# Gated linear attention feeding a squared-ReLU feed-forward layer: ten weight subtractions on GpSimd, three crossing copies on ScalarE, and a new order for the first phase

## The chip, the cores and the metric

One Trainium2 chip, one of its cores. The metric is the device time of one execution in microseconds (us). A core has five engines that run their own queues: TensorE (PE in the rows; its weight loads are PEld), VectorE (DVE), ScalarE (ACT), GpSimd (POOL) and SyncE (SP), which only issues DMAs here. They wait for each other through semaphores.

## The reference

```python
# q, k, v, f_logit: (4 batches, 8 heads, 768 steps, 48), float32
f = 1.0 / (1.0 + np.exp(-f_logit))
for t in range(S):
    state = f[:, :, t, :, None] * state + np.einsum('bhd,bhe->bhde', k[:, :, t], v[:, :, t])
    y[:, :, t] = np.einsum('bhd,bhde->bhe', q[:, :, t], state)
x = y.transpose(0, 2, 1, 3).reshape(3072, 384)
h = x @ w_in                       # 384 -> 2048
r = np.maximum(h, 0.0)
out = (r * r) @ w_out              # 2048 -> 384
```

## The kernel before, in words

Time is cut into 6 blocks of 128 steps, so a block has 512 tokens over the 4 batches. The attention of a block is done in four units, one for each pair of heads; unit n belongs to block n // 4. A unit turns the recurrence into matrix products of 64 steps: VectorE makes running products of the gates with two scans, scales keys and queries by them, and TensorE makes scores, state updates and outputs with many small matmuls. The fourth unit of a block has no keys and queries of its own: heads have 48 rows where a unit has 2 x 64, so the last pair of heads is held in the spare rows of the other three. The output y of a unit is stored as two parts, a high one of the matmul's type (float32r) and the rest, and so are the weights.

The feed-forward layer has 16 slices f of 128 hidden features. For each slice and block, layer 1 is nine matmuls of 128x512 (three input tiles, three products of high and lower parts), then ScalarE does ReLU, square and a copy to the high part `gh`, VectorE subtracts it to get `gl`, and layer 2 is nine matmuls more. The weights come as 64-bit words that are decoded on the chip: two ScalarE passes, a shift-or and a sign-or on VectorE, a ScalarE copy to the high part and a subtraction `w[:, 1] = a - w[:, 0]` for the lower part (`halves`, line 172 copy, line 174 subtraction).

The order of the first phase is written out by hand, in the strings `FIRST` and `SECOND`. Each word is a step, a letter and a number, and `step()` issues it; all instructions of an engine then run in the order of the words. In the first phase the kernel does the attention of blocks 0 and 1 (units 0 to 7), decodes twelve early weights (slices 0 to 5, both layers) and does slices 0 to 5 for block 0. After it a regular flow of 16 slices a block runs. The letters that matter here:

- for a unit: `G` gates (ScalarE, line 446), `K` scan and scaled keys, `Q` the same for queries, `T` four TensorE transposes of the keys, `N` their copy out of PSUM (ScalarE), `S` scores, `D` state updates, `M` the causal mask (VectorE, line 596), `C` the states (VectorE, lines 611 and 618), `Y` the outputs (64 small matmuls, lines 631 and 640), `H` the high part of y (ScalarE, line 660), `z` its subtraction on TensorE (block 0), `X` the lower part (line 674 or 676), `r` and `s` the crossing copies
- the crossing copies: a product of one head may need queries (`rx`, step `r`) and states (`sx`, step `s`) on the other half of the partitions. `across()` (line 486) moves them, by a ScalarE copy or by a DMA of SP's queue. Before, all `r` of block 1 and `s5` to `s7` are DMAs
- `A I V c J` are the five decode steps of a layer-1 weight and `B O Z d P` those of a layer-2 weight. `J` and `P` are the subtractions. `e n t a w` decode the rows of the fourth unit
- `u` is layer 1 for a slice with the first three input tiles, `U` adds the fourth (slices 0 and 1 only) or is the whole (slices 2 to 5), `R` ReLU, square and high part, `E` the lower part (line 264), `W` layer 2 (line 274)
- `g` and `h` move the rows of the fourth unit into the other input tiles, on GpSimd's and SP's DMA queues (line 683); slices 2 and later need them
- `busyN` are N transposes whose result nobody reads (line 805): fill for TensorE

GpSimd does little in this phase: two small maximum steps inside each `K` (line 456), the DMA issues of `m` and `g`, and in the later flow block transposes (line 535). Its queue was not in the set of engines that keep the order by hand, but its order was settled by the tile scheduler.

Of the kernel before, what the change touches and what calls it, by code (L numbers as in the profile page):

```python
# [13 lines left out]
F32 = mybir.dt.float32  # L14
# [29 lines left out]
Q = 32  # L44
# [20 lines left out]
LAST_AT = ((-6, 0, "v"), (1, 1, "s"))  # L65


FIRST = """
j0 e0 n0 f0 busy11 busy3 G0 busy2 k0 t0 K0 T0 f1 k1 Q0 G1 v0 K1 S0 N0 D0 M0 i0 A0 I0 T1 L2 o2 L4 C0
Q1 r0 s0 G2 K2 v1 Y0 N1 H0 z0 X0 D1 S1 B2 i3 Q2 T2 busy3 m1 C1 a0 S2 A3 w0 v2 o1 N2 r1 D2 G4 I3 i1  # L70
M1 s1 K4 v3 A1 Y1 D3 H1 C2 s2 z1 X1 r2 m0 f5 m2 S3 r3 o0 B0 V0 M2 k5 L6 v5 busy3 Y2 H2 Q4 r4 v4 C3 s3
G5 I1 T4 z2 X2 M3 busy9 Y3 c0 N4 K5 G6 Q5 V1 H3 busy5 z3 X3 T5 S4 D4 o3 i5 o5 i2 B3 J0 m4 r5 B1 C4 c1 s4 u0
O0 U0 M4 Y4
"""
SECOND = """
J1 Z0 u1 V3 R0 K6 H4 X4 N5 D5 S5 E0 T6 d0 P0 A2 C5 c3 U1 O1 I2 W0 R1 N6 J3 M5 h3 Z1 d1 s5
Y5 Q6 H5 X5 V2 c2 E1 g3 U3 P1 A5 v6 o4 S6 D6 M6 i4 J2 r6 C6 m5 I5 R3 E3 A4 W1 V5 O3 I4 c5 J5 U2 R2
m6 O2 V4 Z2 s6 v7 r7 Y6 H6 c4 X6 E2 J4 U5 d2 D7 S7 P2 U4 M7 C7 Z3 B4 B5 R4 s7 W2 O4 O5 d3 Z4 Z5 d4
d5 P3 Y7 E4 H7 X7 g7 h7 P4 R5 E5 W3 W4 P5 W5
"""  # L80


class Moe:


    def __init__(self, ctx, tc, const, sums, out):
        self.tc, self.nc, self.sums, self.out = tc, tc.nc, sums, out

        self.const, self.raw, self.w, self.ps, self.turns = const, {}, {}, {}, 0
        self.xs, self.spares, self.w4, self.homes, self.held = [], 0, None, {}, None  # L90

        self.floor = const.tile([P, 1], F32, name="floor")
        tc.nc.vector.memset(self.floor, -31.0 / 64.0)

# [73 lines left out]
        yield from self.halves(self.w[f, i], a)  # L168

    def halves(self, w, a):  # L170
        nc = self.nc
        nc.scalar.copy(out=w[:, 0], in_=a)  # L172
        yield
        nc.vector.tensor_tensor(out=w[:, 1], in0=a, in1=w[:, 0].bitcast(F32), op=ALU.subtract)
        yield

    def decode_any(self, f, i, scr):
# [188 lines left out]
def fast_path(ctx, psum, tc, moe, ident, low, flag, fkqT, vN, w, w4, out):  # L366
    nc = tc.nc
    V, G = nc.vector, nc.gpsimd
# [32 lines left out]
    def weights_load(f, i, mark=False):  # L401
        raw = moe.words(f, i)
        if mark:

            V.memset(raw.bitcast(I32)[0:1, 0:1], 0)
        nc.sync.dma_start(raw, w[f, i])

    class Unit:
# [79 lines left out]
        def crossed(self):  # L488
            self.rx = self.wk([ROWS, B * C], "rx", 2)
            for c in range(self.blk == 0, NC):  # L490
                r = (1 - c) * C
                self.across(
                    self.rx[c * C : c * C + D].rearrange("p (b t) -> p b t", t=C),
                    self.ra[r : r + D].rearrange("p (b c t) -> p b c t", b=B, c=NC)[:, :, c],
                    self.blk == 1,
                )

        def crossed_states(self):
            for c in range(self.blk == 0, NC):
                r = (1 - c) * C  # L500
                self.across(self.sx[c * C : c * C + D], self.sp[r : r + D, c], self.blk == 1 and self.hp > 0)

        def turn(self):

# [26 lines left out]
        def turn_blocks(self):  # L531

            for a in range(0, P, Q):
                for r in range(0, P, Q):
                    ins = G.tensor_copy(  # L535
                        out=self.kn[a : a + Q, :, r : r + Q], in_=self.kb[r : r + Q, :, a : a + Q]
                    ).ins
                    for t in ticks[-1:]:
                        tc.add_manual_dep(ins, t.name, mybir.DependencyInfo(
                            mybir.DependencyClass.NoSync, mybir.DependencyReason.SCHED_ONLY  # L540
                        ), reason="behind the last slot")

        def turned(self):
            if self.n < TURNED:
# [177 lines left out]
    )  # L722
    half = list(range(LO)), list(range(LO, NF))
    xs = {blk: moe.new_x(blk, blk) for blk in range(2)}
    units, decoding, shared, ticks = {}, {}, [], []

    for t in xs[0]:
        G.memset(t[C + 32 :].bitcast(F32), 0.0)
# [10 lines left out]
    def slot(old, new):  # L739

        ab = ps_a.tile([P, 2, 512], F32, tag="ab", name=f"ab{(new or old).nm}_{new is None}")
        rows = [[], []]
        if old:
            old.py = ab[:, :, : B * C]
            for c in range(NC):
                for b in range(B):
                    for part in range(2):  # L750
                        for h in (c, 1 - c):
                            rows[c].append((C, lambda a=(part, b, c, h): old.output_one(*a)))
        if new:
            new.sd = ab[:, :, B * C :]
            new.dd = shared[0].rearrange("p (c e) n -> p c (e n)", c=NC)[:, :, : B * D]
            adds = [
                [] if new.last_of(c) else [
                    (D, lambda a=(b, c, h): update(*a)) for b in range(B) for h in (c, 1 - c)
                ] for c in range(NC)
            ]  # L760
            for h in range(2):
                for b in range(B):
                    for c in (h, 1 - h):
                        rows[h].append((C, lambda a=(b, c, h): new.score_one(*a)))
            rows = [adds[0] + rows[0], rows[1] + adds[1]]
        seen = []

        def behind(ins, first):
            tc.add_manual_dep(ins, first.name, mybir.DependencyInfo(
                mybir.DependencyClass.Sync, mybir.DependencyReason.DATA  # L770
            ), reason="one bank")

        def update(b, c, h):
            ins = new.add_one(new.dd, b, c, h).ins
            if c == 0 and b == B - 1 and h:

                seen.append(G.memset(tick, 0).ins)  # L777
                ticks.append(seen[0])
                behind(seen[0], ins)
            elif c and b == 0 and h:  # L780
                behind(ins, seen[0])

        at = [0, 0]
        while any(rows):
            r = min((r for r in range(2) if rows[r]), key=lambda r: at[r])
            cols, do = rows[r].pop(0)
            at[r] += cols
            do()

    def step(t):  # L790

        nm = t.rstrip("0123456789")
        n = int(t[len(nm) :])  # L800
        if nm == "busy":
            if 0 not in moe.cur.ph:
                moe.bank(0)
            for _ in range(n):
                nc.tensor.transpose(out=moe.cur.ph[0][:, 0:P], in_=ident, identity=ident)
        elif nm in ("i", "o"):
            weights_load(n, "io".index(nm))
        elif nm == "j":
            nc.sync.dma_start(moe.fourth_words(), w4)
        elif nm in "entaw":  # L810
            if nm == "e":
                decoding["fourth"] = moe.decode_fourth()
            next(decoding["fourth"])
        elif nm in "AIVcJBOZdP":
            i = "AIVcJBOZdP".index(nm) // 5
            if nm in "AB":
                decoding[n, i] = moe.decode(n, i, pro, True)
            next(decoding[n, i])
        elif nm == "u":
            moe.up(n, last=False)  # L820
        elif nm == "U" and n < SPLIT:
            moe.up_fourth(n)
        elif nm == "U":
            moe.up(n)
# [12 lines left out]
    pro = early.enter_context(tc.tile_pool(name="pro", bufs=1))  # L837
    minus = pro.tile([ROWS, ROWS], F32R, name="minus")
    nc.scalar.activation(minus, ident[:ROWS, :ROWS], AF.Copy, scale=-1.0)
    with tc.manual_schedule(engines={ET.PE, ET.SP, ET.DVE, ET.Activation}):  # L840
        with tc.tile_pool(name="ps_p", bufs=2, space=bass.MemoryType.PSUM) as ps_p:
            for t in FIRST.split():
                step(t)
# [3 lines left out]
        for t in SECOND.split():  # L847
            step(t)
# [307 lines left out]
```

## Time and profile before

| what | us |
|---|---|
| median of 3 runs (482.86 to 484.52) | 483.9 |
| the profiled execution's own time | 485.53 |
| its span, first to last instruction | 483.8 |
| TensorE busy, 4759 matmuls | 469.5 |
| VectorE busy, 483 instructions | 262.6 |
| ScalarE busy, 561 instructions | 277.4 |
| GpSimd busy, 226 instructions | 84.8 |

The granted clock of TensorE is 0.994 of the full 2.4 GHz over the span. A busy time is the union of an engine's instructions. TensorE's ends are modelled, so instructions overlap in its rows and a wait can lie inside a busy stretch: start-to-start times tell more.

### The profile page before, as it was taken

The page shows a single profiled execution, that of the slowest core. Times are in us where ns is not written, and L with a number is a line of the kernel's source. Part 1 is how long each engine was busy: PE and PEld are TensorE (multiplying, and loading weights), DVE is VectorE, ACT ScalarE, POOL GpSimd, SP SyncE. Part 2 cuts the span into 40 slices and gives each one's busy share as a digit, 9 for nine tenths or more (in the row PEclk, how much of TensorE's full clock was granted, in tenths as well). Part 3 has the DMA queues.
Part 4 walks back from the last instruction along what each step waited for, and adds up shares of the span by engine and source line. Part 5 has one row for each costly group of instructions (what it writes and reads, how often), then busy time and mean ns, then how long its engine had stood idle before and what let it go on. Part 6 is the DMA issues. An engine that isn't in the chain of part 4 may idle for free. (4 is left out here: it accounts for less than half of the span.)

```text
span 483.8 us, 11562 instructions
## 1 busy us (share of the span) xinstructions
PE 469.5 (97%) x4759; PEld 385.8 (80%) x4759; DVE 262.6 (54%) x483; ACT 277.4 (57%) x561; POOL 84.8 (18%) x226
## 2 busy tenths in 40 slices
PE   5888999999999999999999999999999999999996
PEld 5766778888888888888888888888888888888884
DVE  7997995898978447543457453356453312221111
ACT  4785676878758556545546645555654444544441
POOL 6222010001011404150053250052350000000000
PEclk9998999999999999999999999999999999999999
DMA  8983417467204205332005232004300002100002
GB/s 294 311 251 94 131 31 243 161 216 262 60 13 159 84 3 125 95 94 81 3 2 127 94 93 84 1 0 106 114 12 3 2 0 34 66 0 2 1 0 70
DMA packets 22636, 42.60 MB, mean 88 GB/s; under 512 B 4512, under 2 KB 8128, under 8 KB 22576
## 3 DMA queue, kind: packets, MB, share of 16 engines
q1 hardware_dynamic: 22128, 40.86, 27.7%
q0 software_dynamic: 448, 0.92, 0.7%
q8 instruction: 39, 0.64, 0.6%
q14 instruction: 21, 0.17, 0.1%
HBM read 31.69 MB, written 4.72 MB: 75 GB/s over the span
## 5 line engine op out<-in xcount | busy, mean ns | idle before, releaser
L247 PE MATMUL ph<-x,w 128*128 128x512 f32 x864 | 216.3, 395 | 0.0
L247 PEld LDWEIGHTS ph<-x,w 128*128 128x128 f32 x864 | 161.0, 189 | 34.5 <-DVE gl L264 0.3
L274 PE MATMUL po<-gh,w 128*128 128x512 f32 x570 | 175.5, 389 | 0.0
L264 DVE TENSOR_TENSOR gl<-ph,gh 128x512 fp32r<-128x512 f32 x95 | 65.4, 689 | 157.6 <-ACT gh L259 157.3
L257 ACT ACTIVATE ph<-ph 128x512 f32<-128x512 f32 x96 | 55.9, 583 | 127.0 <-PE ph L247 126.8
L274 PEld LDWEIGHTS po<-gh,w 128*128 128x128 f32 x570 | 107.0, 188 | 22.2
L274 PE MATMUL po<-gl,w 128*128 128x512 f32 x285 | 111.2, 390 | 0.0
L274 PEld LDWEIGHTS po<-gl,w 128*128 128x128 f32 x285 | 53.5, 188 | 11.2
L258 ACT ACTIVATE ph<-ph 128x512 f32<-128x512 f32 x96 | 55.9, 582 | 3.0
L259 ACT CAST gh<-ph 128x512 fp32r<-128x512 f32 x95 | 55.8, 587 | 3.0
L535 POOL COPY turn<-turn 32x128 f32<-32x128 f32 x112 | 42.1, 376 | 8.3 <-DVE turn L527 3.7
L456 POOL TENSOR_SCALAR fkq<-fkq 128x8 f32<-128x8 f32 x18 | 12.8, 714 | 141.9 <-DVE fkq L451 119.3
L451 DVE TENSOR_TENSOR_SCAN fkq<-fz,dr 128x520 f32<-128x520 f32 x18 | 22.3, 1238 | 6.7 <-ACT fz L446 6.6
L172 ACT CAST w<-wa 128x384 fp32r<-128x384 f32 (+1 forms) x33 | 16.6, 512 | 14.9 <-DVE wa L159 11.7
L465 DVE TENSOR_TENSOR_SCAN fkq<-fz,dz 128x520 f32<-128x520 f32 x18 | 22.4, 1247 | 0.6
L631 PE MATMUL ab_False<-sc,vn 64*48 64x64 f32 (+1 forms) x480 | 20.7, 220 | 0.0
L676 DVE TENSOR_TENSOR x<-ab_False,x 112x512 fp32r<-112x512 f32 x12 | 8.3, 692 | 21.6 <-ACT x L660 21.6
L660 ACT CAST x<-ab_False 112x512 fp32r<-112x512 f32 x12 | 7.0, 587 | 22.5 <-PE shared L566 17.6
L144 ACT ACTIVATE wa<-raw 128x384 f32<-128x384 f32 (+1 forms) x33 | 18.1, 549 | 2.4 <-DMA raw<-in_w_dram 2.4
L640 PE MATMUL ab_False<-rx,sx 48*48 48x64 f32 (+1 forms) x240 | 19.4, 216 | 0.0
L777 POOL MEMSET flag<- 1x1 int32 x16 | 1.4, 88 | 102.4 <-PE shared L566 100.4
L155 DVE SCALAR_TENSOR_TENSOR wa<-raw,wa 128x384 int32<-128x384 int32 (+1 forms) x33 | 18.0, 552 | 0.7
(148 smaller groups left out, 499.3 us busy)
## 6 DMA issues: line engine op xcount, KB each, us to landing
raw<-in_w_dram SPq DMA_DIRECT2D x32, 384.0 KB, 3.8
fkq<-in_fkqT_dram SPq DMA_DIRECT2D x15, 768.0 KB, 5.4
vn<-in_vN_dram SPq DMA_DIRECT2D x24, 192.0 KB, 4.7
out_dram<-ob SPq DMA_DIRECT2D x14, 256.0 KB, 2.2
fkq<-in_fkqT_dram SPq DMA_DIRECT2D x9, 256.0 KB, 4.5
x<-ys SPq DMA_DIRECT2D x30, 64.0 KB, 2.3
last_kq<-fkq SPq DMA_DIRECT2D x28, 64.5 KB, 2.3
out_dram<-part SPq DMA_DIRECT2D x3, 256.0 KB, 2.6
```

The costliest lines, as they stand in the source:

```text
L144: nc.scalar.activation(a, upper_f, AF.Abs, scale=2.0**-112, **kw)
L247: self.nc.tensor.matmul(self.cur.ph[f], lhsT=w[:, i], rhs=x[:, j], start=first and n == 0, stop=last and n == 2)
L257: nc.scalar.activation(ph, ph, AF.Relu)
L258: nc.scalar.activation(ph, ph, AF.Square)
L259: nc.scalar.copy(out=gh, in_=ph)
L264: self.nc.vector.tensor_tensor(out=gl, in0=self.cur.ph.pop(f), in1=gh.bitcast(F32), op=ALU.subtract)
L274: self.nc.tensor.matmul(c.po[e], lhsT=l, rhs=r, start=f == c.fs[0] and i == 0, stop=f in c.ends and i == 2, skip_group_check=len(c.ends) > 1,)
L451: V.tensor_tensor_scan(out=rr[:, ::-1], data0=self.fz[:, NZ * CZ : 0 : -1], data1=dr[:, ::-1], initial=0.0, op0=ALU.mult, op1=ALU.add,)
L465: V.tensor_tensor_scan(out=pp, data0=self.fz[:, : NZ * CZ], data1=dz, initial=0.0, op0=ALU.mult, op1=ALU.add)
L535: ins = G.tensor_copy(out=self.kn[a : a + Q, :, r : r + Q], in_=self.kb[r : r + Q, :, a : a + Q]).ins
L631: nc.tensor.matmul(to[:m], lhsT=self.vn[rows, b, h * D : h * D + m], rhs=self.sc[rows, h, b], start=b == 0, stop=none and c == 0 and b == ...
L640: nc.tensor.matmul(to[:m], lhsT=s[rows, b * D : b * D + m], rhs=q[rows], start=False, stop=b == B - 1,)
```

## The change

Three things are changed. First, `BY_POOL` names ten of the twelve early subtractions, and `step()` lets GpSimd do them (`moe.less`). GpSimd joins the engines whose order is kept by hand, and a scheduling hint that held its block transposes behind a marker goes. Second, `BY_DMA` names the crossings that stay DMAs, `r5 r6 s6 r7`; so `r4`, `s5` and `s7`, two copies each, are done by ScalarE. Third, `FIRST` and `SECOND` have the steps in another order, with 19 fill transposes where there were 36. After the first phase the order of all queues is that of before.

```diff
+BY_DMA = ("r5", "r6", "s6", "r7")
+
+BY_POOL = ("J0", "P0", "J1", "P1", "J2", "P2", "J3", "P3", "J5", "P5")
+
 FIRST = """
-j0 e0 n0 f0 busy11 busy3 G0 busy2 k0 t0 K0 T0 f1 k1 Q0 G1 v0 K1 S0 N0 D0 M0 i0 A0 I0 T1 L2 o2 L4 C0
...
+j0 e0 f0 busy3 n0 t0 k0 G0 busy2 K0 a0 f1 T0 G1 k1 w0 v0 N0 Q0 K1 Q1 D0 S0 M0
...
     def halves(self, w, a):
-        nc = self.nc
-        nc.scalar.copy(out=w[:, 0], in_=a)
+        self.nc.scalar.copy(out=w[:, 0], in_=a)
         yield
-        nc.vector.tensor_tensor(out=w[:, 1], in0=a, in1=w[:, 0].bitcast(F32), op=ALU.subtract)
+        self.less.tensor_tensor(out=w[:, 1], in0=a, in1=w[:, 0].bitcast(F32), op=ALU.subtract)
         yield
...
-                    self.blk == 1,
+                    f"r{self.n}" in BY_DMA,
...
-                self.across(self.sx[c * C : c * C + D], self.sp[r : r + D, c], self.blk == 1 and self.hp > 0)
+                self.across(self.sx[c * C : c * C + D], self.sp[r : r + D, c], f"s{self.n}" in BY_DMA)
...
+            moe.less = G if t in BY_POOL else V
             next(decoding[n, i])
+            moe.less = V
...
-    with tc.manual_schedule(engines={ET.PE, ET.SP, ET.DVE, ET.Activation}):
+    with tc.manual_schedule(engines={ET.PE, ET.SP, ET.DVE, ET.Activation, ET.Pool}):
```

The first place is ScalarE around the fourth unit's high part `H3` (the first CAST into `ys0_3`), up to the first slice's ReLU. In names such as `fkq1_2_494` the first two numbers are block and pair of heads, and `wa3_0` is slice 3, layer 1. Before:

```order
L172 CAST w0_0_582<-wa0_0_232 128x384
L546 COPY kn1_0_584<-pk1_0_539 128x448
L548 COPY last_kn_78<-pk1_0_539 128x8x16
L446 ACTIVATE fz1_72<-fkq1_2_494 128x8x64
L660 CAST ys0_3_596<-first_py_125 112x2x4x64
L674 CAST ys0_3_596<-first_py_125 112x2x4x64
L144 ACTIVATE wa3_1_652,sums_60<-raw3_1_644 128x384
```

And of the change, from the same place to the states' crossing:

```order
L151 ACTIVATE wa0_1_534,sums_60<-raw0_1_444 128x384
L153 ACTIVATE raw0_1_444<-raw0_1_444,floor_62 128x384
L660 CAST ys0_3_567<-first_py_125 112x2x4x64
L178 CAST w1_0_577<-wa1_0_433 128x384
L674 CAST ys0_3_567<-first_py_125 112x2x4x64
L151 ACTIVATE wa3_0_580,sums_60<-raw3_0_320 128x384
L151 ACTIVATE wa2_1_583,sums_60<-raw2_1_231 128x384
L546 COPY kn1_1_639<-pk1_1_588 128x448
L548 COPY last_kn_78<-pk1_1_588 128x8x16
L492 COPY rx1_0_674<-fkq1_0_257 48x256 x2
L492 COPY sx0_75<-sp0_73 48x208 x2
L452 ACTIVATE fz1_72<-fkq1_2_531 128x8x64
```

The gates of unit 6 (`fz1_72`, step `G6`) stood ahead of `H3` and now stand behind the copies; `B0`, the start of weight 0 of layer 2, is ahead of `H3`; and `rx1_0` (step `r4`) is a ScalarE copy here where it was a DMA of SP.

The second place is GpSimd's queue from the fourth block-1 key step on. Before:

```order
L476 DMA last_kq_77<-fkq1_1_462 16x1032
L456 TENSOR_SCALAR fkq1_2_494<-fkq1_2_494 128x8
L456 TENSOR_SCALAR low_59<-fkq1_2_494 128x8
L683 DMA x0_0_116<-ys0_3_596 16x1024
L683 DMA x0_1_117<-ys0_3_596 16x1024
L683 DMA x0_2_118<-ys0_3_596 16x1024
```

And of the change:

```order
L180 TENSOR_TENSOR w1_0_577<-wa1_0_433,w1_0_577 128x384
L482 DMA last_kq_77<-fkq1_0_257 16x1032 x2
L482 DMA last_kq_77<-fkq1_1_390 16x1032 x2
L462 TENSOR_SCALAR fkq1_2_531<-fkq1_2_531 128x8
L462 TENSOR_SCALAR low_59<-fkq1_2_531 128x8
L180 TENSOR_TENSOR w0_1_738<-wa0_1_534,w0_1_738 128x384
L683 DMA x0_0_116<-ys0_3_567 16x1024
L683 DMA x0_1_117<-ys0_3_567 16x1024
L683 DMA x0_2_118<-ys0_3_567 16x1024
L180 TENSOR_TENSOR w3_0_772<-wa3_0_580,w3_0_772 128x384
L180 TENSOR_TENSOR w2_0_865<-wa2_0_742,w2_0_865 128x384
```

The subtractions (`TENSOR_TENSOR`) stand among the key steps and the DMA issues; `P0` (`w0_1`) is ahead of the three issues of `g3`.

## Rows read from the trace of the kernel before

**Rows 1.** The page: busy us (share of the span) and instructions.
```profile
PE 469.5 (97%) x4759; PEld 385.8 (80%) x4759; DVE 262.6 (54%) x483; ACT 277.4 (57%) x561; POOL 84.8 (18%) x226
```

**Rows 2.** Stretches: length, busy us of each engine, granted clock, DMA share, GB/s.
```profile
20.50:37.50 17.00, 14.75 (x378) 12.10 (x378) 16.13 (x30) 14.25 (x35) 3.97 (x8) 1.00 0.87 257
37.50:40.90 3.40, 2.01 (x67) 1.50 (x65) 3.22 (x5) 1.75 (x3) 0.73 (x1) 1.00 0.27 61
40.90:44.40 3.50, 3.50 (x16) 2.47 (x10) 2.02 (x4) 3.08 (x8) 1.26 (x3) 0.58 0.21 40
44.40:56.00 11.60, 11.22 (x224) 8.87 (x224) 9.10 (x18) 6.54 (x14) 0.48 (x1) 0.98 0.48 137
56.00:70.00 14.00, 14.00 (x237) 11.09 (x236) 13.42 (x30) 10.90 (x25) 0.00 (x0) 1.00 0.14 36
```

**Rows 3.** Timeline of TensorE: start, us, instruction, [idle before, and what ended it].
```profile
11.67 1.09 PE L513 MATMUL pk<-ident,fkq 128*128 128x128 f32 x4
...
31.62 0.77 PE L805 MATMUL ph<-ident 128*128 128x128 f32 x5
...
33.22 0.60 PE L513 MATMUL pk<-ident,fkq 128*128 128x128 f32 x4
...
35.13 2.33 PE L247 MATMUL ph<-x,w 128*128 128x512 f32 x9
37.30 0.86 PE L247 MATMUL ph<-ys,w 112*128 112x512 f32 x3
...
39.92 0.36 PE L640 MATMUL py<-rx,sx 48*48 48x64 f32 x3 [1.39 <-DMA rx<-fkq]
...
40.98 3.82 PE L247 MATMUL ph<-x,w 128*128 128x512 f32 x9
...
67.69 0.34 PE L631 MATMUL py<-sc,vn 64*64 64x64 f32 x8
```

**Rows 4.** ScalarE: the crossing copies of line 486, then its timeline.
```profile
L486 ACT COPY sx<-sp x6: 363/364/364, 13.1 to 37.1; 48x208 f32<-48x208 f32 x6
L486 ACT COPY rx<-fkq x3: 403/403/403, 11.5 to 26.0; 48x256 f32<-48x256 f32 x3
...
31.73 0.63 ACT L446 ACTIVATE fz<-fkq 128x512 f32<-128x512 f32 x1 [0.82 <-DMA fkq<-in_fkqT_dram]
32.26 0.57 ACT L660 CAST ys<-first_py 112x512 fp32r<-112x512 f32 x1
33.42 0.58 ACT L674 CAST ys<-first_py 112x512 fp32r<-112x512 f32 x1 [0.58 <-PE first_py L666]
34.04 0.58 ACT L144 ACTIVATE wa<-raw 128x384 f32<-128x384 f32 x1
...
35.16 0.53 ACT L144 ACTIVATE wa<-raw 128x384 f32<-128x384 f32 x1
```

**Rows 5.** Timeline of VectorE from `M3` (line 596) on.
```profile
28.97 0.68 DVE L596 TENSOR_TENSOR sc<-ds,mask 128x512 f32<-128x512 f32 x1
29.57 1.23 DVE L451 TENSOR_TENSOR_SCAN fkq<-fz,dr 128x520 f32<-128x520 f32 x1
...
31.66 0.21 DVE L463 RECIPROCAL dz<-fkq 128x8 f32<-128x8 f32 x1
...
33.78 0.55 DVE L155 SCALAR_TENSOR_TENSOR wa<-raw,wa 128x384 int32<-128x384 int32 x1
...
34.72 0.35 DVE L611 TENSOR_TENSOR sp<-state,fkq 112x192 f32<-112x192 f32 x1
```

**Rows 6.** Timeline of GpSimd and VectorE, at 23 and at 245 us.
```profile
23.21 0.74 POOL L456 TENSOR_SCALAR fkq<-fkq 128x8 f32<-128x8 f32 x1 [5.38 <-DVE fkq L451]
...
244.79 0.28 POOL L535 COPY turn<-turn 32x128 f32<-32x128 f32 x1
...
245.06 1.24 DVE L465 TENSOR_TENSOR_SCAN fkq<-fz,dz 128x520 f32<-128x520 f32 x1
245.12 1.27 POOL L535 COPY turn<-turn 32x128 f32<-32x128 f32 x1
```

More of the change, by code (lines that the diff above doesn't have):

```diff
@@ L65 @@
 LAST_AT = ((-6, 0, "v"), (1, 1, "s"))
+BY_DMA = ("r5", "r6", "s6", "r7")
+BY_POOL = ("J0", "P0", "J1", "P1", "J2", "P2", "J3", "P3", "J5", "P5")
 FIRST = """
-j0 e0 n0 f0 busy11 busy3 G0 busy2 k0 t0 K0 T0 f1 k1 Q0 G1 v0 K1 S0 N0 D0 M0 i0 A0 I0 T1 L2 o2 L4 C0
[L70 to L73, printed above, removed]
+j0 e0 f0 busy3 n0 t0 k0 G0 busy2 K0 a0 f1 T0 G1 k1 w0 v0 N0 Q0 K1 Q1 D0 S0 M0
+i0 L2 r0 o2 r1 S1 T1 L4 C0 busy6 G2 m0 v1 A0 m1 s0 N1 K2 T2 Y0 G4 H0 I0 Q2
+i3 V0 D1 N2 v2 z0 S2 o1 i1 D2 M1 X0 C1 v3 f5 m2 K4 s1 Y1 C2 B1 H1 z1 r2
+A1 T4 busy3 o0 D3 M2 s2 O1 X1 Y2 G5 Q4 S3 c0 r3 J0 H2 I1 N4 M3 z2 X2 k5 C3
+L6 s3 B0 V1 Y3 busy5 H3 v5 z3 K5 c1 X3 A3 B2 v4 T5 J1 S4 m4 o3 D4 O0 Q5 M4
+i5 N5 o5 u0 i2 C4
 """
 SECOND = """
[L76 to L79, printed above, removed]
+m5 U0 r4 s4 G6 Y4 Z0 u1 I3 K6 R0 V3 H4 v6 d0 X4 P0 A2 U1 r5 Z1 o4 E0 D5
+c3 I2 g3 S5 T6 C5 h3 B5 W0 M5 V2 s5 R1 J3 Y5 Q6 c2 H5 N6 X5 d1 i4 A5 U3
+r6 J2 S6 E1 I5 D6 v7 C6 A4 R3 O5 V5 s6 M6 O2 E3 U2 m6 c5 P1 R2 Z2 Z5 d2
+I4 W1 Y6 r7 V4 H6 d5 X6 J5 U5 S7 c4 J4 E2 B4 O4 D7 C7 B3 s7 U4 O3 Z3 d3
+Z4 P2 M7 P5 R4 P3 E4 W2 d4 Y7 W3 P4 H7 X7 R5 g7 W4 E5 h7 W5
 """
@@ L90, in __init__ @@
         self.xs, self.spares, self.w4, self.homes, self.held = [], 0, None, {}, None
+        self.less = tc.nc.vector
         self.floor = const.tile([P, 1], F32, name="floor")
@@ L534, in turn_blocks @@
                 for r in range(0, P, Q):
[L535 to L541, printed above, removed]
+                    G.tensor_copy(out=self.kn[a : a + Q, :, r : r + Q], in_=self.kb[r : r + Q, :, a : a + Q])
         def turned(self):
@@ L724, in fast_path @@
     xs = {blk: moe.new_x(blk, blk) for blk in range(2)}
-    units, decoding, shared, ticks = {}, {}, [], []
+    units, decoding, shared = {}, {}, []
     for t in xs[0]:
@@ L777, in update @@
                 seen.append(G.memset(tick, 0).ins)
-                ticks.append(seen[0])
                 behind(seen[0], ins)
```

## The prediction

> **What bounds the kernel now.** I read the stretches first, because shares of the whole span hide where the time can still move. TensorE is busy for 469.5 of 483.8 us [rows 1], but a pipelined matmul counts as busy while it waits, so this says little. By stretches [rows 2], from 56 to 70 us TensorE has no idle time at all, and the page's slices stay full behind that: there TensorE is the bound. From 20.5 to 37.5 us it is the other way: VectorE works 16.1 of 17 us, ScalarE 14.3, TensorE 14.8 with its fill matmuls counted in. The early part is bound by the chain that makes x for block 0, and the end of the kernel moves with the moment from which TensorE runs without a break.
>
> That moment shows in TensorE's order of time [rows 3]. The first real layer-1 product, `u0`, starts at 35.13 us. Its nine matmuls and the three of `U0` are issued by 38.1. Then `Y4` (the attention output of unit 4) stands still for 1.39 us until 39.92, and the profile names the DMA of `rx` as what ended it. `u1` starts at 40.98, and its nine matmuls take 3.82 us where those of `u0` take 2.33. The granted clock explains it: 0.58 on average from 40.9 to 44.4 us, so the lower level (1.2 GHz) for most of that, after a stretch from 37.5 to 40.9 in which TensorE was busy for 2.01 of 3.40 us [rows 2]. After that there are only small holes: 0.38 us idle between 44.4 and 56.
>
> So what this change can win lies mostly between 35 and 44.4 us. After it, TensorE's work is fixed and the order in all five queues is the old one.
>
> **The change, part by part.** *Crossing copies.* `r4`, `s5` and `s7` leave SP's queue and go to ScalarE: two `rx` copies at 0.403 us and four `sx` copies at 0.364 us [rows 4], 2.26 us more for ScalarE. What it removes is the DMA for which `Y4` waited: 1.39 us on the path. On SP six issues fall away, so what stands behind them is issued no later. In the new order `r4` and `s4` (already on ScalarE) stand after `A3` and `B2`, the starts of two weight decodes, and `N5`. From the end of `X3` at about 34.0 us that is 1.1 + 1.1 (the spacing of two such starts in [rows 4]) + 0.8 + 0.81 + 0.73 = 4.5 us, so `sx` is complete near 38.5, about when `U0` is through. I take a residual wait of 0.2, bounds 0 to 1.0.
>
> *First part of the order, up to `u0`.* Ahead of `M3`, VectorE's queue loses one weight step (`I3`) and `C3`, and gains `O1`. A weight step takes 0.47 us from start to start (two of them from 33.78 to 34.72), a two-instruction `C3` some 0.7 [rows 5]: 0.7 us less. On ScalarE `G6`, which waited 0.82 us for its load ahead of `H3` [rows 4], goes behind `s4`: at most 0.8 won. Against that, `T2` now stands ahead of `Y0` on TensorE, so unit 0 is finished only after `K2`, and `B0` (1.1 us) stands ahead of `H3`. These cancel within what the rows can tell, and I keep `u0` at 35.1, bounds 1.5 us either way.
>
> *Sum to `u1`.* It started 40.98 - 35.13 = 5.85 us after `u0`. Without the 1.39, and with the residual 0.2 already part of that, it starts some 4.1 to 4.3 us after: **1.7 us** earlier. If TensorE has no long hole before it, the clock stays at its upper level and `u1` takes 2.33 instead of 3.82: another **1.5 us**. Bounds for this term are 0 and 1.7.
>
> *Fill.* 36 fill transposes become 19. The five ahead of `z3` took 0.77 us [rows 3], but each group stands ahead of a step that waits for another engine, as `z3` does for `H3`. At the upper clock, taking 17 out gives nothing while those waits stay. What it costs if the cover goes is a rival below.
>
> *Subtractions.* Ten of twelve `w = a - high` go from VectorE to GpSimd: 10 x 0.47 = 4.7 us off VectorE's queue. How long GpSimd needs for 128x384 with two inputs no row shows. Its copy of 128 elements takes 0.28 us alone, but 1.27 us when it starts beside VectorE's scan [rows 6]; it ended 0.09 us after the scan did. Likewise its 128x8 step took 0.74 us from 23.21 although it has hardly anything to do. So GpSimd waits while VectorE reads two operands. Three times the elements at the lone copy's price make 0.84 us; I take 0.9, with 0.4 below it (some of the 0.28 is fixed) and 1.5 above (the blocked copy and a little). GpSimd has room: between 44.4 and 70 it is busy for under 0.5 us [rows 2]. Of what waits for it, `P0` stands ahead of `g3`, whose transfers into x `U3` needs. I price that and the other new small waits at 0.5 us, and the old holes after 44.4 that go at the same.
>
> Does VectorE keep up if TensorE arrives earlier? From `M3` to `M7` the new queue holds 21 weight steps (9.9 us at 0.47), two `K` and two `Q` (4 x 2.1), five masks (0.6 each), `C3` to `C7` (6.3), and seven PSUM evictions like a mask in size (4.2): 31.8 us by [rows 5]. From 28.9 this ends at 60.7; `M7` is wanted when `Y7` starts, at 67.69 - 3.2 = 64.5 [rows 3]. There are 3.8 us to spare.
>
> Here a rule speaks against the change. The rows come first: GpSimd's copy is drawn out to the end of VectorE's scan [rows 6]; that VectorE waits for GpSimd no long GpSimd instruction of this trace shows. The Trainium skill ("SBUF — State Buffer", section "Who interferes with whom") says that a VectorE instruction with two SBUF inputs and a GpSimd instruction that reads SBUF exclude each other, and that whichever issues second waits for all of the first; the row agrees for one of the two directions. The Trainium skill ("GPSIMD Engine Reference", section "Performance versus the Vector engine") gives 4497 ns for 2048 elements, so 0.84 us for 384 by my estimate, and by both pages VectorE would lose up to 8.4 us to save 4.7.
>
> **Sum.** The profiled execution took 485.53 us (span 483.83). 1.7 + 1.5 + 0.5 - 0.5 = 3.2 us: 482.3. The median of the three runs, 483.9, lies 1.6 below that execution, so against it I forecast **480.7 us**.
>
> **Rivals.** *VectorE loses the shared reads (slower).* Each subtraction holds up VectorE's next two-input step, and most of its queue is such steps. For: [rows 6] show the two engines excluding each other, and VectorE was busy for 13.4 of the 14 us from 56 to 70. Against: so far it was always GpSimd that waited. It decides from about 0.5 us for each of the eight subtractions between `M3` and `M7`, where the 3.8 us are used up. At 0.9 to 1.1 us each they add 8 us at most: `M7` ends at 60.7 + 8 = 68.7, and with the waits of `X4` for `H4` (0.6) near 69.3, so `Y7` comes 1.6 us later than at 67.69: 485.5 us.
>
> *The clock stays low early.* Four transposes took 1.09 us at 11.67 and 0.60 at 33.22 [rows 3], so by the durations alone the array ran at about half rate at first. The first fill was 16 and becomes 5. If the rate rises only late, the outputs, scores and transposes of units 0 to 2, some 6 us of work at the full rate in the chain to `M3`, cost up to 3 us more. With the 3.2 won: 483.7 us. If the fall at `u1` comes back as well, 485.2.
>
> *Nothing is left of it.* ScalarE has 2.3 us more work ahead of evictions in a stretch where it was 84% busy, so the wait for `rx` turns into a wait for ScalarE of the same length, and the clock falls at `u1` as before: 483.9 us.
>
> **How the numbers follow.** About 0.3% (1.45 us) is what a measurement can tell here. The forecast gets 0.57 with its own range of 478.6 to 482.3; the shared reads 0.17, the late clock 0.15 (half of it within 0.3%, the rest slower or faster), nothing 0.11. That makes faster 0.61, the same 0.19, slower 0.20. The range reaches from 478.2, where `u0` also gains and no hole replaces an old one, to 485.6, the price of the shared reads.
>
> **What would show it.** Right: `Y4` without a wait for a DMA, `u1` starting near 39.2 us and taking 2.3 us, no stretch at the lower level after 35 us, ten subtractions on GpSimd near 0.9 us each, and no idle TensorE after 45 us. Wrong: `u0` later than 36.6 us, masks or evictions by which TensorE waits for VectorE between 50 and 68 us, two-input VectorE steps that grow from 0.55 us, or a `U3` that waits for the transfers behind `P0`. If the steps up to `Y7` are early but the kernel isn't, I have mistaken what bounds the part after 70 us.

## The result and the profile after

The change took **487.62 us** (median of seven, 484.08 to 489.17), the kernel before, measured beside it, 483.41 (482.66 to 484.52): ratio 1.0081, 95% interval [1.0056, 1.0106]. It is slower, by 0.8%, where I forecast faster by 0.7%. The profiled execution of the change is the shortest of its seven: 484.08 us, span 482.3. That is the first thing to see: its trace shows the change when nothing goes wrong, and the median is 3.5 us longer.

Line numbers from here on are mostly of the changed kernel, a few lines on from the old ones: L247, L274, L486 and L513 of before are L253, L280, L492 and L519. The stretches of the profile after, with the columns of [rows 2]:

```profile
20.50:37.50 17.00, 13.71 (x385) 11.30 (x376) 15.95 (x28) 16.27 (x40) 7.21 (x10) 1.00 0.83 268
37.50:40.90 3.40, 3.37 (x73) 2.56 (x72) 3.14 (x6) 3.29 (x8) 0.73 (x1) 1.00 0.70 184
40.90:44.40 3.50, 3.50 (x78) 2.82 (x77) 3.50 (x6) 3.03 (x9) 3.34 (x5) 1.00 0.42 72
44.40:56.00 11.60, 10.71 (x163) 8.34 (x161) 11.19 (x22) 9.84 (x23) 4.42 (x5) 1.00 0.37 87
```

TensorE's order of time in the same trace, as in [rows 3]:

```profile
14.00 1.14 PE L582 MATMUL ds<-fkq 48*64 48x64 f32 x32 [2.27 <-DVE fkq L474]
15.06 1.11 PE L519 MATMUL pk<-ident,fkq 128*128 128x128 f32 x4
...
31.45 0.33 PE L631 MATMUL first_py<-sc,vn 64*48 64x64 f32 x8 [0.17 <-issue]
...
32.94 0.60 PE L519 MATMUL pk<-ident,fkq 128*128 128x128 f32 x4
...
34.85 2.35 PE L253 MATMUL ph<-x,w 128*128 128x512 f32 x9
...
39.34 2.34 PE L253 MATMUL ph<-x,w 128*128 128x512 f32 x9
...
47.03 0.50 PE L631 MATMUL py<-sc,vn 64*64 64x64 f32 x5 [0.89 <-DVE sc L596]
```

In this execution the steps that I named come out: `u0` at 34.85, no wait of `Y4`, `u1` at 39.34 and 2.34 us long, granted clock 1.00 in all four stretches. The 0.89 us ahead of `Y5` is new. GpSimd's ten subtractions, with smallest, median and largest duration in ns:

```profile
L180 POOL TENSOR_TENSOR w<-wa,w x10: 1016/1210/1975, 28.0 to 64.5; 128x384 fp32r<-128x384 f32 x10
```

They are longer than the 0.9 I took, and two are above my upper bound of 1.5. VectorE pays too. Five of its two-input steps in this trace, where the medians are 0.69 us for `L474`, 0.55 for `L156` and 0.36 for `L611`:

```profile
34.25 1.32 DVE L474 TENSOR_TENSOR fkq<-fkq 128x512 f32<-128x512 f32 x1
...
36.09 0.34 DVE L611 TENSOR_TENSOR sp<-state,fkq 112x192 f32<-112x192 f32 x1
...
42.79 0.76 DVE L156 SCALAR_TENSOR_TENSOR wa<-wa,raw 128x384 int32<-128x384 int32 x1
43.48 1.16 DVE L611 TENSOR_TENSOR sp<-state,fkq 112x192 f32<-112x192 f32 x1
...
45.14 0.76 DVE L611 TENSOR_TENSOR sp<-state,fkq 112x192 f32<-112x192 f32 x1
```

And GpSimd at the same times, as in [rows 6]:

```profile
33.05 1.98 POOL L180 TENSOR_TENSOR w<-wa,w 128x384 fp32r<-128x384 f32 x1
...
41.43 1.71 POOL L180 TENSOR_TENSOR w<-wa,w 128x384 fp32r<-128x384 f32 x1
43.08 1.54 POOL L683 DMA_DIRECT2D x<-ys  x3
44.64 1.03 POOL L180 TENSOR_TENSOR w<-wa,w 128x384 fp32r<-128x384 f32 x1
```

The steps at 34.25, 42.79 and 45.14 us stand beside a subtraction and end 0.2 to 0.5 us after it. So now both directions are seen: GpSimd waits for VectorE's scan [rows 6], and VectorE waits for GpSimd. That agrees with the Trainium skill ("SBUF — State Buffer", section "Who interferes with whom").

The step at 43.48 is less plain. It takes 1.16 us beside the three DMA issues of `g3`, not beside a subtraction, and ends at 44.64, when the next subtraction, `J3`, begins. With `J3` back on VectorE (run j3dve, below) the same step beside the same issues is short:

```profile
43.47 1.54 POOL L683 DMA_DIRECT2D x<-ys  x3
43.86 0.34 DVE L611 TENSOR_TENSOR sp<-state,fkq 112x192 f32<-112x192 f32 x1
```

So `J3` holds it up, and not the issues; how it can before its record begins is not shown.

### The profile page after: what moved, and what is told of

It is laid out like the page before. It is cut to its first block, busy times and chain, and to the rows that moved or that the text cites. A ratio compares the mean times of both kernels' runs of the same rounds, so it can differ in the third digit from the quotient of the medians.

```text
span 482.3 us, 11531 instructions
## 1 busy us (share of the span) xinstructions
PE 463.0 (96%) x4742; PEld 381.1 (79%) x4742; DVE 261.4 (54%) x473; ACT 279.6 (58%) x567; POOL 98.5 (20%) x236
## 5 line engine op out<-in xcount | busy, mean ns | idle before, releaser
L253 PE MATMUL ph<-x,w 128*128 128x512 f32 x864 | 214.9, 393 | 0.1
L253 PEld LDWEIGHTS ph<-x,w 128*128 128x128 f32 x864 | 160.0, 188 | 34.3 <-DVE gl L270 0.3
L280 PE MATMUL po<-gh,w 128*128 128x512 f32 x570 | 175.5, 389 | 0.0
L280 PEld LDWEIGHTS po<-gh,w 128*128 128x128 f32 x570 | 107.0, 188 | 22.2
L280 PE MATMUL po<-gl,w 128*128 128x512 f32 x285 | 111.1, 390 | 0.0
L280 PEld LDWEIGHTS po<-gl,w 128*128 128x128 f32 x285 | 53.5, 188 | 11.1
L162 DVE SCALAR_TENSOR_TENSOR wa<-raw,wa 128x384 int32<-128x384 int32 (+1 forms) x33 | 19.0, 580 | 0.8
```

The source lines that it names most:

```text
L162: nc.vector.scalar_tensor_tensor(out=h, in0=upper, scalar=-(1 << 31), in1=h, op0=ALU.bitwise_and, op1=ALU.bitwise_or)
L253: self.nc.tensor.matmul(self.cur.ph[f], lhsT=w[:, i], rhs=x[:, j], start=first and n == 0, stop=last and n == 2)
L280: self.nc.tensor.matmul(c.po[e], lhsT=l, rhs=r, start=f == c.fs[0] and i == 0, stop=f in c.ends and i == 2, skip_group_check=len(c.ends) > 1,)
```

## Does the long time repeat, and where does it begin?

Three runs of the change, nothing edited. 

> The changed kernel once more, nothing altered, for more executions with span and clock of each. Clock theory: the executions spread over 483 to 489 us as before, and the long ones have the lower granted clock (0.986 to 0.991), the short ones 0.996 or more. Shared-reads theory: the times spread no more than those of the kernel before (2 us), or spread without the clock moving with them.

Measured: 486.09 us (483.2 to 490.59, 12 runs), ratio 1.0053 [1.0021, 1.0084], taken without the longest. The loss is real and so is the spread; of 58 runs of the kernel before, measured beside this run and the next ones, all stay within 482.2 to 487.5 and 57 within 485.9.

> The changed kernel once more, for the trace of another execution. Clock theory: if it is a long one (over 486 us), its trace shows a stretch at the lower level of the granted clock between 20 and 40 us, and u0 starts after 37 us; if a short one, none, and u0 near 35 us. The flow of 16 slices takes the same time in either.

> As the run before it: one more execution of the changed kernel, the same expectation.

The first, again2, was a short execution (483.52 us, span 481.8), the second, again3, a long one (487.91, span 486.2). That gave a pair of traces of one program. The first matmul of the regular flow starts at 71.59 and 75.94 us, and the spans differ by as much: behind it nothing is lost or won. All of the difference arises between 20 and 36 us. TensorE in the long one:

```profile
21.67 0.56 PE L582 MATMUL ds<-fkq 48*64 48x64 f32 x19
23.33 0.39 PE L582 MATMUL ds<-fkq 48*64 48x64 f32 x11 [1.10 <-issue]
...
27.54 1.05 PE L519 MATMUL pk<-ident,fkq 128*128 128x128 f32 x4
...
35.60 0.33 PE L631 MATMUL first_py<-sc,vn 64*48 64x64 f32 x8 [1.17 <-issue]
...
38.99 2.33 PE L253 MATMUL ph<-x,w 128*128 128x512 f32 x9
```

and its stretches, with the granted clock third from the right:

```profile
20.50:23.50 3.00, 1.58 (x57) 1.18 (x50) 2.46 (x4) 2.84 (x8) 0.00 (x0) 1.00 0.50 152
23.50:27.00 3.50, 2.77 (x94) 2.56 (x90) 2.34 (x5) 1.11 (x3) 0.97 (x2) 0.54 0.83 268
27.00:30.50 3.50, 3.50 (x60) 3.17 (x63) 2.74 (x5) 3.42 (x8) 0.00 (x0) 0.50 0.87 256
```

`u0` starts at 38.99 against 34.85 in the profile after, 4.14 us later, and the two traces side by side account for it: 0.18 are there when the scores of unit 2 (`S2`) begin; 1.10 is a wait in the middle of `S2` that ends with "issue", the profile's word where it shows nothing that TensorE waited for; 1.87 are lost up to `z2`, where the granted clock is at its lower level (1.2 GHz) and four transposes take 1.05 us instead of 0.60; and 1.00 is a second wait of that sort in `Y3` (1.17 against 0.17).

## The first theory: fill and the clock

My rival *the clock stays low early* now led: the change has less fill, TensorE is idle for 4.35 and 2.27 us ahead of `T0` and `S1`, and by this theory the clock rises late and falls again. Fill was put back into the new order, and taken out of the old one.

```diff
 fill (fillearly: the first two lines alone; filllate: the last three alone)
-j0 e0 f0 busy3 n0 t0 ...      +j0 e0 f0 busy17 n0 t0 ...
-... r1 S1 T1 ...              +... r1 busy8 S1 T1 ...
-... B1 H1 z1 r2               +... B1 H1 busy3 z1 r2
-... O1 X1 Y2 ...              +... O1 X1 busy4 Y2 ...
-... B0 V1 Y3 ...              +... B0 V1 busy5 Y3 ...
 lessfill (the kernel before)
-j0 e0 n0 f0 busy11 busy3 ...  +j0 e0 n0 f0 busy3 ...
-... M3 busy9 Y3 ...           +... M3 busy3 Y3 ...
```

> The changed kernel with 37 more fill transposes, put where TensorE waits in the first 31 us (17 instead of 3 at the start, 8 before S1, 3 before z1, 4 before Y2, 5 before Y3). Clock theory: the spread closes, the granted clock is 0.996 or more in nearly all executions, and the median falls from about 488 to 482 or 483 us. Shared-reads theory: 487 to 488 us as the change, since fill moves nothing on VectorE or GpSimd.

> The kernel before with 17 fill transposes fewer (3 instead of 14 at the start, 3 instead of 9 before Y3), nothing else. Clock theory, if fill alone is what holds the clock: slower than before by 2 to 4 us with a spread of some 5 us and clocks under 0.992. If the new order is what leaves TensorE idle: within 1 us of before. Shared-reads theory: as before.

> The changed kernel with only the 22 early ones of the 37 added fill transposes (14 at the start, 8 before S1). Clock theory, first form (the clock's first rise comes too late and the outputs of units 0 to 2 run at the lower level): as with all the fill, 483 to 484 us and no spread. Second form (the clock falls again between 20 and 35 us because TensorE idles there): no better than the change, 486 to 488 us, spread 6 us.

> The changed kernel with only the 12 late ones (3 before z1, 4 before Y2, 5 before Y3). Clock theory, second form: 483 to 484 us and no spread. First form: as the change, 486 to 488 us with a spread of 6 us.

| run | us, median (range, runs) | ratio to before [95%] |
|---|---|---|
| fill, 37 transposes more | 483.5 (483.14 to 483.95, 11) | 1.0000 [0.9990, 1.0010] |
| fillearly, 22 | 483.51 (482.94 to 484.86, 12) | 0.9989 [0.9971, 1.0006] |
| filllate, 12 | 484.96 (482.94 to 488.8, 12) | 1.0032 [1.0009, 1.0055] |
| lessfill, old order, 17 fewer | 483.15 (482.51 to 484.74, 12) | 0.9991 [0.9977, 1.0005] |

The 22 early transposes remove the loss and the spread. But three things did not fit a theory of the clock. The old order does not need them: lessfill has as little fill at the start as the change. The granted clock of the run with all the fill is as poor early on as one could fear, without costing anything:

```profile
10.00:20.50 10.50, 10.07 (x198) 8.86 (x198) 9.96 (x15) 4.28 (x11) 4.25 (x8) 0.54 1.05 349
```

(In the profile after this column reads 1.00 for the same stretch, although sets of four transposes take 1.11 us there, as at the lower level; so early on the durations tell.) And by durations the clock rises no later in the change than before it. The 32 scores of one unit take 1.13 us at the lower level and 0.69 at the upper; from the kernel before, lessfill and the profile after, in this order:

```profile
20.55 0.87 PE L582 MATMUL ds<-fkq 48*64 48x64 f32 x32
21.37 1.13 PE L582 MATMUL ds<-fkq 48*64 48x64 f32 x32
21.49 0.69 PE L582 MATMUL ds<-fkq 48*64 48x64 f32 x32
```

lessfill, where the rise comes last, is not slow. So a late first rise is not the cause; whether the later fall is, stays open here.

lessfill also tells what the two large terms of my sum were. In the kernel before with fewer transposes TensorE goes

```profile
37.62 0.86 PE L247 MATMUL ph<-ys,w 112*128 112x512 f32 x3
38.42 0.34 PE L631 MATMUL py<-sc,vn 64*64 64x64 f32 x8
...
39.55 2.34 PE L247 MATMUL ph<-x,w 128*128 128x512 f32 x9
```

from `U0` through `Y4` to `u1` without the 1.39 us for `rx`, and `u1` takes 2.34 us, though `rx` still comes by DMA.

## Subtractions, crossings, and the holes that are left

```diff
 nopool, fillnopool
-BY_POOL = ("J0", "P0", "J1", "P1", "J2", "P2", "J3", "P3", "J5", "P5")
+BY_POOL = ()
 fillcross
-BY_DMA = ("r5", "r6", "s6", "r7")
+BY_DMA = ("r4", "r5", "s5", "r6", "s6", "r7", "s7")
```

nopool is the change with all twelve subtractions on VectorE; fillnopool and fillcross have the fill of the run fill as well. 

> The changed kernel with all twelve subtractions back on VectorE; order, crossings and fill as changed. Shared-reads theory: VectorE is no longer held up, the median falls by 3 us or more, to 484 or below. Clock theory: the same spread and the same low clocks as the change, the median within 1.5 us of it (486 to 489).

> The changed kernel with all added fill and with the twelve subtractions on VectorE. Shared-reads theory in its strong form (a subtraction on GpSimd costs VectorE as much as it saves): within 1 us of the same kernel with GpSimd's subtractions (483.5). If GpSimd's subtractions relieve VectorE by 4.7 us less some 3 us of waits, and this order needs that: 486 to 488 us, with TensorE waiting for lower parts of weights (line 180) after 55 us.

> The changed kernel with all added fill and with r4, s5 and s7 as DMAs again. If the 1.39 us wait of Y4 for the DMA of rx is there in every execution, 1.4 us slower than with ScalarE's copies (485). If it came from one execution with a late transfer: within 0.5 us of 483.5.

Measured: nopool 493.86 us (488.44 to 495.56, 6 runs), ratio 1.0174 [1.0128, 1.0220], above what either theory forecast; fillnopool 488.45 (486.29 to 490.23, 6), 1.0081 [1.0056, 1.0106]; fillcross 483.66 (483.37 to 484.24, 12), 0.9998 [0.9987, 1.0009]. Three things follow. The crossing copies on ScalarE are worth nothing that can be measured (fillcross against fill). GpSimd's subtractions are worth 5.0 us in this order (488.45 against 483.5), so the rival *VectorE loses the shared reads* falls as a cause. And since the order with them is no faster than the kernel before, the order without them costs what they bring. Most of that cost is a wait of the products for lower parts of weights that VectorE has not yet subtracted. In fillnopool, who waited for whom, from 40 to 75 us (total us, times, longest):

```profile
PE po L280 <- DVE w L180: 3.2, 2, 2.5
PE ph L253 <- DVE w L180: 1.5, 1, 1.5
```

With GpSimd's subtractions (short22, below) no such wait is left in this window.

Two runs, both with the early fill, tried to gain from the hole ahead of `Y5`. j3dve gives `J3` back to VectorE; j3b2 also moves `B2` behind `A4`.

```diff
 j3dve
-BY_POOL = ("J0", "P0", "J1", "P1", "J2", "P2", "J3", "P3", "J5", "P5")
+BY_POOL = ("J0", "P0", "J1", "P1", "J2", "P2", "P3", "J5", "P5")
 j3b2, besides
-... X3 A3 B2 v4 ...     +... X3 A3 v4 ...
-... C6 A4 R3 ...        +... C6 A4 B2 R3 ...
```

> The changed kernel with the 22 early fill transposes and one subtraction, J3, back on VectorE. Shared-reads theory: the states of unit 5 (line 611) take 0.35 us again instead of 1.16, M5 is earlier, the 0.9 us hole of TensorE ahead of Y5 closes, and the time falls by 0.3 to 0.9 us below 483.5. If that hole has another cause, 483.5.

> The same with B2, the start of a weight decode on ScalarE, moved from ahead of r4 to behind A4. If Y4's wait of 0.7 us is ScalarE's queue ahead of s4, it closes and the time falls by another 0.5 us or so, to 482 to 483. If the later decode of that weight makes W2 or R3 late: no gain or up to 1 us slower.

Measured: j3dve 483.19 us (482.33 to 484.96, 12 runs), 0.9994 [0.9978, 1.0009]; j3b2 483.71 (482.62 to 486.52, 12), 1.0009 [0.9989, 1.0029]. The hole ahead of `Y5` goes, but the next thing is late: in j3b2 `U3` waits for the rows of the fourth unit,

```profile
48.29 3.91 PE L253 MATMUL ph<-x,w 128*128 128x512 f32 x9 [1.90 <-DMA x<-ys]
```

so neither is clearly faster than the kernel before.

## The second theory: the ends of TensorE's instruction blocks

The waits with "issue" had stayed unexplained. Each matmul has a number here by its start in the trace, from 0. In again, again3 and nopool, which have one and the same stream of TensorE, the first such wait stands ahead of matmul 220 and a second one ahead of 472. The row of the first

```profile
21.76 0.39 PE L582 MATMUL ds<-fkq 48*64 48x64 f32 x11 [0.49 <-issue]
```

is from again; nopool has

```profile
24.04 0.59 PE L582 MATMUL ds<-fkq 48*64 48x64 f32 x11 [2.28 <-issue]
```

In the kernel before, whose order is another, they stand ahead of matmuls 347 and 473:

```profile
24.57 0.33 PE L566 MATMUL ds<-vn,last_kn 64*48 64x48 f32 x6 [0.67 <-issue]
...
30.92 0.25 PE L640 MATMUL first_py<-last_kq,sp 48*48 48x64 f32 x1 [0.42 <-issue]
```

So they lie at steps of 126 matmuls (94, 220, 346, 472; an early record more or less shifts them by one), whatever stands there. The "issue" waits of all other traces of this case fit too: the only further places are 599 and 850. With its weight load a matmul is two instructions, 252 together. The page of the profile lists a queue that brings instructions,

```profile
q8 instruction: 39, 0.64, 0.5%
```

39 transfers, 16 KB each by the trace's records of them. Set beside each other, for the block that begins at matmul 220 (times in us; matmul 94 by the start of its weight load, transfers by the records of that queue):

| run | matmul 94 | transfer | wait ahead of 220, until | end of transfer to go-ahead |
|---|---|---|---|---|
| after (short) | 14.49 | 18.14 to 19.22 | none, reached at 21.7 | |
| again2 (short) | 14.41 | 18.09 to 19.54 | none, reached at 21.7 | |
| again | 14.46 | 18.85 to 20.11 | 0.49, 21.76 | 1.65 |
| again3 | 14.69 | 20.68 to 21.85 | 1.10, 23.33 | 1.48 |
| nopool | 14.28 | 21.25 to 22.54 | 2.28, 24.04 | 1.50 |
| lessfill | 13.90 | 18.28 to 19.36 | none, reached at 21.9 | |
| fillearly | 13.39 | 15.23 to 16.31 | none, reached at 19.2 | |

Where TensorE waits it goes on about 1.5 us after the transfer's end; where the transfer ended earlier than that, there is no wait. In the two short executions of the change the margin is 0.7 and 1 us, and the transfer, which starts 3.6 to 7 us after matmul 94 in this stream, comes late by more than that in others. The Trainium skill ("Runtime: NRT & Kernel Launch", section "Instruction fetch mechanics") states that instructions are streamed in 16 KiB blocks of 256 while the block before runs, and that a crossing is mostly hidden. The block size agrees with the 126 matmuls, which take 252 of the 256 places. Most crossings are hidden here too, but up to three in an execution are not: in the rows above they took up to 2.28 us of TensorE's time.

Early fill thus did two things: it kept TensorE at work, and it moved every later matmul 22 places, so that block ends fell elsewhere and matmul 94 came a microsecond earlier. The last six runs part them.

```diff
 small    22 more matmuls 48x64 by 64 columns: 14 behind busy3, 8 ahead of S1
+nc.tensor.matmul(ph[0:C, 0:C], lhsT=ident[0:D, 0:C], rhs=ident[0:D, 0:C], ...)
 small2   the same 22 behind T2, ahead of Y0
 long     busy3 and busy2 at the start, and 2 of the 6 ahead of T2 (now ahead of S1), as
+nc.tensor.matmul(ph as P x 2 x P, lhsT=ident, rhs=ident twice, ...)
 short22  the 22 places of small, each
+nc.tensor.transpose(out=ph[0:32, 0:32], in_=ident[0:32, 0:32], identity=ident[0:32, 0:32])
 short22nopool   short22 with BY_POOL = ()
 wlate    the change with two loads later
-... r0 o2 r1 S1 ... i3 V0 ... v3 f5 m2     +... r0 r1 S1 ... V0 ... v3 f5 i3 o2 m2
```

> The change with 22 more matmuls of 48x64 by 64 columns where the early fill had its 22 transposes (14 behind the first fill, 8 ahead of S1). They move the place of every later matmul in TensorE's stream by 22, as the early fill did, but are far shorter. Two theories of the 2 to 7 us by which most executions of the change are late. (a) Code: in the traces of the change TensorE stood without a named cause ahead of matmul 220 of its stream (0.49, 1.10 and 2.28 us) and went on 1.5 to 1.65 us after the end of a 16 KB instruction transfer; that transfer began 3.6 to 7.0 us after matmul 94 of the stream, at 14.4 us, and 1.9 after it in the kernels with early fill, where it stood at 13.2. The small matmuls bring matmul 94 ahead of S1, to 11 to 12 us, so the transfer comes some 3 us earlier and no such wait is left: 483.5 us, nothing over 485. (b) Clock: TensorE is as idle as in the change up to 14 us, its granted clock rises near 20 us and falls back in many executions: 486 us, spread 483 to 490.

> The change with its five fill transposes at the start replaced by five matmuls of 256 columns in four passes (an estimate of 0.85 us each at the half clock, from the 0.23 us of a 128-column transpose), two of the six ahead of T2 put ahead of S1 in the same form, so TensorE is busy about as long at the start as with the early fill, and from Y0 on every matmul has the place in the stream that it has in the change, unless such a matmul takes more than one place, which the place of the waits will show. (a) Code: matmul 94 still stands in S1 near 14.4 us, the instruction transfer still starts at 18 to 21 us, and the waits ahead of matmul 220 stay: 485.5 to 486.5 us with executions over 487. (b) Clock: the granted clock rises as early as with the early fill (6 to 14 us), no execution is long: 483.5 us. If the times lie between, both count.

> The change with the 22 small matmuls behind T2, ahead of Y0. (a) Code: matmul 94 is where it was, near 14.4 us, so the transfer starts as late as in the change, and matmul 220 now is the second of z0, some 0.5 us earlier than before: the waits stay or grow by up to 0.5 us: 486 us, executions over 487. If instead only the place matters at which the block ends (ahead of S2, where TensorE waits for the high part of y anyway), 483.5. (b) Clock: a little more work just ahead of the rise of the clock: as the change, 486 us, at most 0.5 better.

> The change with 22 transposes of 32x32 (one place each in the stream) where the early fill had its 22 of 128x128: 14 at the start, 8 ahead of S1. The run small moved the stream by 44 places, not 22, because a float32 matmul takes two, and its wait stood ahead of matmul 347 of the stream; this one moves it by 22 as the early fill did. (a) Code: matmul 220 falls at z0 and 347 into the steps ahead of M2 where the early-fill run showed no wait; TensorE reaches matmul 94 at 13 us or before, the instruction transfer starts by 16 us, no wait without a cause over 0.3 us up to u0: 483.5 us (up to 484.5), nothing over 486. (b) Clock: TensorE works less at the start than with the early fill, its clock rises near 20 us and falls in many executions: 486 us, spread 483 to 490.

> The same 22 short transposes with all twelve subtractions on VectorE. Without fill that kernel took 493.86 us (its trace has the longest code wait, 2.28 us ahead of matmul 220, and three stretches at the half clock), with all the fill 488.45. (a) Code: the wait goes and the clock stays: 488.5 us, at most 490. (b) Clock: as without fill, 493 to 494.

> The change with nothing altered on TensorE: only the loads of two weights that are wanted late (i3 and o2, 384 KB each, decoded from 33 us on) are issued behind the load f5, so at 21 us, where they were issued by 11 us. (a) Code, in full: the transfer of the second instruction block waits in the DMA engines behind those loads; with 768 KB fewer ahead of it (2.2 us at the 350 GB/s of the stretch from 10 to 20.5 us) it starts 1 to 2 us sooner, 14.5 to 17 us, and the waits ahead of matmul 220 are gone: 483.5 us, without executions over 486; below 483 if the key and value loads that now land sooner let TensorE start T0 or D0 sooner as well. (b) Clock: nothing is changed for TensorE's clock before 14 us: 486 us with the spread of the change, 485 if the earlier loads gain 1 us by themselves. If i3 or o2 comes too late now, TensorE or ScalarE waits for raw ahead of A3 or B2, and the time is over 486 in every execution.

| run | us, median (range, runs) | ratio to before [95%] |
|---|---|---|
| small | 486.79 (485.57 to 487.53, 6) | 1.0068 [1.0047, 1.0090] |
| long | 486.06 (483.03 to 489.41, 12) | 1.0064 [1.0032, 1.0097] |
| small2 | 490.2 (489.92 to 491.18, 5) | 1.0147 [1.0124, 1.0169] |
| short22 | 483.45 (482.84 to 485.35, 12) | 0.9999 [0.9984, 1.0015] |
| short22nopool | 488.05 (486.71 to 489.2, 6) | 1.0092 [1.0067, 1.0117] |
| wlate | 485.22 (482.95 to 487.41, 12) | 1.0031 [1.0011, 1.0050] |

*long* has the work without the shift (a plain float32 matmul turned out to take two places, so the shift is 7, and matmul 220 still lies in `S2`). Its clock has the same poor stretch as that of fill,

```profile
10.00:20.50 10.50, 9.71 (x186) 7.74 (x179) 9.83 (x15) 4.28 (x11) 4.25 (x8) 0.55 1.05 350
```

and yet fill has no long execution and long has five of twelve over 488. Work alone cures nothing.

*short22* has the shift almost without the work. Its sets of four transposes are as slow as those of the change up to 17.25 us at least, so the clock had not risen by then, where with early fill the set at 14.78 us takes 0.66:

```profile
7.25 1.11 PE L519 MATMUL pk<-ident,fkq 128*128 128x128 f32 x4 [3.23 <-DVE fkq L463]
...
14.98 1.11 PE L519 MATMUL pk<-ident,fkq 128*128 128x128 f32 x4
...
17.25 1.09 PE L519 MATMUL pk<-ident,fkq 128*128 128x128 f32 x4
...
20.95 0.69 PE L582 MATMUL ds<-fkq 48*64 48x64 f32 x32
...
34.08 2.37 PE L253 MATMUL ph<-x,w 128*128 128x512 f32 x9
```

Still it takes 483.45 us, as the early fill does, with no "issue" wait of TensorE up to `u1`; and the same in the kernel without GpSimd's subtractions takes 493.86 to 488.05. Both are what the second theory forecast and 2.5 and 5 us from the clock's. The place of the block ends is the cause of the loss; filllate, which leaves matmul 220 where it was, keeps its long executions. That the fall of the clock is a consequence fits again3, where it falls 0.4 us after the wait ahead of matmul 220, but is not shown. In the trace of j3dve, which has no "issue" wait, the clock is low as well, behind a wait of 0.84 us for a mask (granted clock third from the right):

```profile
29.50:36.50 7.00, 6.86 (x117) 6.08 (x116) 6.34 (x9) 5.62 (x15) 3.84 (x7) 0.51 0.90 321
```

That execution took 483.52 us, 0.3 above the median of its kernel. So the clock falls on other occasions too, and without making an execution long. Nor does each late block do so: fill's trace has a wait of 0.90 us ahead of 599, inside `u0`, and took 483.62 us.

*small*, forecast at 483.5 by the second theory, took 486.79. It is no test of 22 places, because its matmuls take two each (22 issued, 44 in the trace). But it moved the wait where the numbers say: matmul 347,

```profile
24.35 0.32 PE L631 MATMUL first_py<-sc,vn 64*48 64x64 f32 x6 [1.02 <-issue]
```

1.53 us after the end of the transfer from 21.74 to 22.82. *small2* is inconclusive: its small matmuls took 4.85 us ahead of `Y0`, on the path. *wlate* went against its forecast of 483.5. In its trace the transfer started no earlier with 768 KB less ahead of it (18.39 us; 18.09 to 20.68 in the four traces of the change), so nothing shows those two loads holding it back. Behind the place where the loads went, at 20 to 21 us, the next two blocks came late, whether for that reason or not:

```profile
26.29 0.33 PE L566 MATMUL ds<-vn,last_kn 64*64 64x48 f32 x8 [0.96 <-issue]
...
33.22 0.46 PE L631 MATMUL first_py<-sc,vn 64*48 64x64 f32 x8 [2.61 <-issue]
```

1.53 and 1.42 us after the transfers that ended at 24.76 and 31.80. Why a transfer takes 2 to 7 us from matmul 94 to its start stays open; the DMA engines were full up to 20.5 us (share 1.05), but contention there is not shown, and wlate gives no sign of it.

## Why the prediction was wrong

**Subtractions.** Sized low (median 1.21 us for 0.9, worst 1.98 above the bound of 1.5), and VectorE lost time as the rival said. The weighing was right: VectorE kept up but for the 0.89 us ahead of `Y5`, and without GpSimd the order is 4.6 to 5.0 us slower.

**Crossing copies.** The wait of 1.39 us went, but in fillcross, with the crossings as DMAs, it is gone too.

**Sum to `u1`, and the sum.** The 1.7 us do not follow from their own figures: 5.85 less 1.39 is 4.46 us, and with the residual of 0.2 it is 4.66, so 1.2 to 1.4 us earlier. (In the profile after `u1` starts 4.49 us after `u0`.) And both terms, 1.7 and 1.5 us, were taken from one execution that lay 1.6 us above the median, and I then moved the sum to the median. What probably made that execution long was counted as what the change would win; no trace of a short execution of the kernel before is there to show it. In lessfill, the same order with less fill, neither wait nor low clock is there, and the regular flow starts at 71.55 us; in the short executions of the change at 71.59 and 71.89. The change's own gain is nil: short22, the change without its loss, stands at 483.45 us, 0.9999 [0.9984, 1.0015] to before. So of the 6.9 us between forecast and result, 2.7 are the gain that is not there, and 4.2 go with the place of the block ends (2.6 by the twelve executions of again).

**Fill, the step that failed.** "At the upper clock, taking 17 out gives nothing while those waits stay": I priced the transposes as work, and their second effect, as places in the instruction stream, not at all. The rival of a late clock had the sign (483.7 or 485.2) but not the mechanism; 487.62 lies above every case I worked out, and the rise that it feared is not later than before. The trace of before held the warning, in the two "issue" waits of 0.67 and 0.42 us that I passed over because the rows name no releaser.

**What would show it.** "`u0` later than 36.6 us" was the right alarm for long executions: 38.99 in again3.

No version run is clearly faster than the kernel before; the lowest ratios are 0.9989 [0.9971, 1.0006] (fillearly) and 0.9991 [0.9977, 1.0005] (lessfill). Not tried: the old order with its block ends at 347 and 473 moved into places where TensorE waits anyway.

## What to carry to other kernels

Before a sum is made from one profiled execution, compare its time with the other runs of the same kernel: waits that only a long execution has are not the change's to win. When TensorE waits for nothing that the profile names, number its matmuls; waits at equal steps are block ends of its instruction stream, and then adding or removing matmuls or transposes moves them, and a late block costs most in the chain that the rest waits for. To learn what fill does, part its work from its number: the same number of tiny instructions, and the same work in fewer.

## What was unexpected of the hardware

A block of 16 KB of TensorE's instructions, 126 matmuls with their weight loads, can be late early in the kernel: the waits shown above are 0.17 to 2.61 us, and TensorE goes on 1.26 to 1.65 us after the transfer's end. A plain float32 matmul takes two places in that stream, a float32 transpose one. In again3 a wait of 1.10 us was followed by 6.8 us at the lower level of the granted clock, which lost 1.87 us more, and by a second late block (1.00): 4 us in all.
